# A first product by seven block products in the second half, groups of four feature tiles, and block sums kept in DRAM

## The chip, the cores and the metric

The program runs on one core of one Trainium2 chip. A core has a matrix engine (TensorE, "PE" in the profile; its weight loads are "PEld"), a vector engine (DVE), a scalar engine (ACT), GpSimd (POOL), the queue engine SyncE (SP) and 16 DMA engines. The metric is the device time of one execution in microseconds (us). A matmul is named by what streams through the array: "128x512" is a matmul of 512 columns, whose 128x128 stationary operand has been loaded by an LDWEIGHTS of its own.

## The reference, cut to what matters

```python
xn = layernorm(x)                                   # x = A_q, [2048, 576]
# conv branch
for t in range(4):                                  # short causal convolution of k, per channel
    k_shift += k_pad[:, t:t + S, :] * shift_k[:, 3 - t]
kv = k_shift * v
y = irfft(rfft(kv, 4096) * rfft(ssm_k, 4096))[:2048] + kv * ssm_D
branch_a = xn * y
# dense branch
h = relu(xn @ w1)                                   # w1 [576, 4608]
branch_b = h @ w2                                   # w2 [4608, 576]
return x + branch_a + branch_b
```

All of it is fp32. The kernel writes an operand of a matrix product as a sum of a high and a low part, and makes the product as three matmuls, high x high, high x low and low x high, that add up in one PSUM group.

## The kernel before, in words

**Dense branch.** The 2048 rows are four blocks of 512, two per half, and each half goes through all of W1 and W2. The 4608 features are 12 chunks of three feature tiles of 128 (`FT = 3`). For a chunk and a block, `mm1` (line 334) makes one feature tile of h, transposed, from 14 matmuls of 512 columns: 4 x 3 for the first 512 of the 576 input features, and 2 for the last 64, whose high and low part lie stacked on 128 partitions. ACT then writes the high part of relu(h) (`hh`, line 339), and DVE the low part (`ll`, line 340). `mm2` (line 358) takes 128 rows and 288 output columns: 9 matmuls (three feature tiles, three products) make one PSUM group, which DVE adds to the sum in SBUF (`acc`, line 362 for block 0, whose rows take 1/std on the way, line 366 for the others). That is 384 such adds. The weights come by DMA (`r`, lines 288 to 297); ACT makes their high parts (lines 306 and 315), POOL the low ones (line 277).

**The rows of the second half** are loaded, normalised and transposed by `make_xT` (line 269) in the last chunk of the first half, about 500 us into the program.

**Conv branch.** `conv` (line 408 on) is a generator that runs beside the dense branch: four stages of a long FFT, here called fk (the filter's first stage, lines 392 to 399), fx (the short convolution and the signal's first stage), fm (both second stages, the product and the way back, lines 553 to 617) and fo (the last stage and the gate, lines 656 to 703). In fx, each of 16 steps takes on DVE: one multiply by the first tap (line 483), three multiplies `e` (line 486), three adds (line 487), the gate by v (line 492), and two stacked splits `xs` (line 392), and for these the matmuls `psf<-xs` (line 398, 8 of 288 columns per step). ACT takes these out of PSUM (line 399).

**What sets the order.** There is one instruction stream for each engine. `tick(cost)` is called after each few matmuls of the dense branch. It counts their columns and, when the conv branch is behind its share, takes the generator's next step. A step yields its weight (`W_FK`, `W_FX`, `W_FM`, `W_FO`), or a negative number, which is a pause in columns of dense work. So these weights say how many dense matmuls stand between two conv matmuls. Each engine then takes its instructions strictly in this order and waits on semaphores. `here()` and `issue_after` set an instruction's place on ACT and DVE behind a named one.

**SP's queue.** It issues nearly all loads in program order. The filter comes in 16 loads `kt` (line 421) of 64 partitions x 36 x 32 elements with runs of 128 bytes, spaced by `KT_GAP` in columns of dense work. The weights of the next chunks lie among them.

Of the kernel before, what the change touches and what calls it, by code (L numbers as in the profile page):

```python
# [17 lines left out]
P = 128  # L18
# [8 lines left out]
FT = 3  # L27
FC = FT * P
NCHUNK = DFF // FC
# [15 lines left out]
W_MM1 = 14 * 512  # L45
W_MM2 = FT * 6 * NH
PAUSE = 16000
START = 4000
PAUSES = 16
SHARE = 0.985  # L50
# [3 lines left out]
W_FK, W_FX, W_FM, W_FO = 1.4, 4.1, 1.26, 2.4  # L54
KD = 36
KT_GAP = 6000
FFT_TOTAL = N_FK * W_FK + N_FX * W_FX + N_FM * W_FM + N_FO * W_FO

SPLITS = {(0, 1): ((1, 0),), (0, 2): ((1, 1),), (1, 0): ((1, 2), (2, 0)), (1, 1): ((2, 1),),
          (1, 2): ((2, 2),)}  # L60
SPLITS0 = {(1, 0): ((1, 0), (1, 1)), (1, 1): ((1, 2), (2, 0)), (1, 2): ((2, 1), (2, 2))}
FFN_TOTAL = NCHUNK * NB * (FT * W_MM1 + BT * W_MM2)

# [45 lines left out]
def h3_ffn_kernel(ctx: ExitStack, tc, x, k, v, shift_k, ssm_k, ssm_D, w1, w2, fwd, inv, mid, out):  # L109
# [8 lines left out]
    hp = ctx.enter_context(tc.tile_pool(name="hp", bufs=2 * FT))  # L118
    xp = ctx.enter_context(tc.tile_pool(name="xp", bufs=2))
    dram = ctx.enter_context(tc.tile_pool(name="dram", bufs=1, space=DRAM))  # L120
    ps_h = ctx.enter_context(tc.tile_pool(name="ps_h", bufs=2, space=PSUM))
# [11 lines left out]
    fin = dram.tile([HT // 2, P, 2, D], F32, name="fin")  # L133

# [21 lines left out]
    def load_x(t, tag, bufs, **queues):  # L156
        pair = xp.tile([P, 2, D], F32, tag=tag, name=f"{tag}{t}", bufs=bufs)
        move(pair, x, slice(t, t + 2), **queues)
        return pair

    def load_acc(t, **queues):
        pairs[t] = load_x(t, "acc", HT // 2, **queues)
        acc[t], acc[t + 1] = pairs[t][:, 0, :], pairs[t][:, 1, :]
# [27 lines left out]
    xT = {}  # L191
    done = {}

    def xT_tiles(b):
        hi = xp.tile([P, 4, 512], F32R, tag="xhi", name=f"xhi{b}")
        lo = xp.tile([P, 4, 512], F32R, tag="xlo", name=f"xlo{b}")
        hl = xp.tile([P, 512], F32R, tag="xhl", name=f"xhl{b}")
        xT[b] = (hi, lo, hl)

    def split_x(b, c, ps):  # L200
        hi, lo, hl = xT[b]
        if c < 4:
            last = nc.scalar.activation(hi[:, c, :], ps, AF.Copy)
            nc.vector.tensor_tensor(lo[:, c, :], ps, hi[:, c, :], OP.subtract)  # L204
            return last
        else:
            done["act"] = nc.scalar.activation(hl[:64, :], ps[:64, :], AF.Copy)
            done["dve"] = nc.vector.tensor_tensor(hl[64:, :], ps[:64, :], hl[:64, :],
                                                  OP.subtract)

    def first_xT(srcs):

        xT_tiles(0)
# [4 lines left out]
        behind = None  # L218
        for t in range(BT):
            if t % 2 == 0:  # L220
                pair = xp.tile([P, 2, D], F32, tag="xn", name=f"xn{t}", bufs=BT // 2)
            xn = pair[:, t % 2, :]
# [13 lines left out]
        for c in range(5):  # L236
            last = split_x(0, c, ps[c])
            if c == 1:
                with tc.issue_after(last.ins):
                    split_w1(0, 1)  # L240
# [5 lines left out]
    def make_xT(b, srcs, in_place=False):  # L246

        xT_tiles(b)
        t0 = b * BT
        for t in range(t0, t0 + BT):  # L250
            at = done["acc"] if in_place else lows[2 * (t - t0) // BT]
            with tc.issue_after(at.ins):
                stats(t, srcs[t])
        with tc.issue_after(at.ins):
            inv_std(t0, BT)
        xn = []
        for t in range(t0, t0 + BT):
            if in_place:
                xn.append(srcs[t])
            else:  # L260
                if t % 2 == 0:
                    pair = xp.tile([P, 2, D], F32, tag="xn", name=f"xn{t}", bufs=BT // 2)
                xn.append(pair[:, t % 2, :])
            normalized(xn[-1], srcs[t], t)
        for c in range(5):
            w = min(P, D - c * P)
            ps = fft_psum()
            for i in range(BT):
# [576 lines left out]
```

## Time and profile before

| | |
|---|---|
| time, median of 3 runs | 1087.06 us (1085.4 to 1087.46) |
| span of the profiled execution | 1084.4 us |
| TensorE matmuls | 1070.8 us busy, 6537 instructions |
| TensorE weight loads | 977.2 us busy |
| VectorE | 732.5 us busy, 1213 instructions |
| ScalarE | 585.0 us busy, 1184 instructions |
| GpSimd | 261.9 us busy, 218 instructions |
| granted TensorE clock | 0.997 |
| moved by DMA | 150.79 MB |

The profiled execution's span lies 2.7 us under the median of the runs. Matmuls overlap in the records (a record is longer than the distance from one start to the next), so a matmul's cost is read from start to start, and the busy share of PE says only that PE nearly always had a matmul under way. The page's parts by line and by wait name a helper's line where one records many operations; lines 392 and 398 each serve two stages, and the tile's name (ks or xs) tells them apart.

### The profile page before, as it was taken

What the parts mean: (1) busy time and instruction counts of PE and PEld (TensorE: products, weight loads), DVE (VectorE), ACT (ScalarE), POOL (GpSimd) and SP (SyncE); (2) the same over time, 40 slices, a digit from 0 to 9 for tenths busy, and PEclk for the clock granted to TensorE, in tenths of its full rate; (3) what the DMA queues carried; (4) which work ended last, traced back from release to release, by engine and by line L of the source; (5) the groups of instructions that cost most, each with busy time, mean ns of one, the idle gap of its engine ahead of it and who ended that gap; (6) DMA issues with size and microseconds to landing.
All of it is one profiled execution on the core that took longest, in us unless ns stands there. A gap on an engine that the chain in (4) does not pass through costs nothing.

```text
span 1084.4 us, 17301 instructions
## 1 busy us (share of the span) xinstructions
PE 1070.8 (99%) x6537; PEld 977.2 (90%) x6537; DVE 732.5 (68%) x1213; ACT 585.0 (54%) x1184; POOL 261.9 (24%) x218
## 2 busy tenths in 40 slices
PE   8999999999999999999999999999999999999998
PEld 5889899998999999999999999899999999999998
DVE  5423677949998777677666676666656666876774
ACT  4221587823443323333388787888788864543430
POOL 4131222412312322312213031211113032332410
PEclk9999999999999999999999999999999999999999
DMA  9950345664644525325564343434344227745524
GB/s 217 181 145 27 119 147 190 195 185 133 187 138 136 153 77 164 117 60 171 190 182 135 99 135 99 135 99 136 92 143 141 80 103 221 201 130 143 164 81 110
DMA packets 112255, 150.79 MB, mean 139 GB/s; under 512 B 45261, under 2 KB 62927, under 8 KB 112172
## 3 DMA queue, kind: packets, MB, share of 16 engines
q1 hardware_dynamic: 103884, 135.50, 42.0%
q0 software_dynamic: 7968, 13.44, 4.8%
q8 instruction: 52, 0.85, 0.3%
q10 hardware_dynamic: 320, 0.74, 0.3%
q14 instruction: 31, 0.25, 0.1%
HBM read 114.26 MB, written 35.39 MB: 138 GB/s over the span
## 4 chain that ended last, share of the span: by engine, by line
PE 90%; DMA 4%; SPq 2%; DVE 2%; ACT 1%; issue 1%; POOL 0%; ACTq 0%; DVEq 0%
PE pso L358 40%; PE psh L334 39%; PE psf L562 7%; PE psf L398 3%; DMA r<-in_w 3%; SPq L421 2%; PE psf L700 1%; PE psf L701 1%; DMA k-1_2414<-in_k 1%; DMA sk<-in_shift_k 0%; PE psf L269 0%; DVE lok L553 0%; POOL l L277 0%; DVE k L611 0%; DVE lox L553 0%
## 5 line engine op out<-in xcount | busy, mean ns | idle before, releaser
L277 POOL TENSOR_TENSOR l<-r,h 128x640 fp32r<-128x640 f32 (+1 forms) x144 | 224.4, 1563 | 621.8 <-ACT h L306 448.3
L358 PE MATMUL pso<-h,hh 128*128 128x288 f32 x1152 | 337.3, 295 | 3.7 <-ACT hh L339 2.7
L358 PE MATMUL pso<-l,hh 128*128 128x288 f32 x1152 | 338.5, 295 | 0.0
L358 PE MATMUL pso<-h,ll 128*128 128x288 f32 x1152 | 337.7, 295 | 0.0
L334 PE MATMUL psh<-xhi,h 128*128 128x512 f32 x576 | 226.5, 394 | 1.1 <-DVE ll L340 1.1
L334 PE MATMUL psh<-xlo,h 128*128 128x512 f32 x576 | 226.5, 393 | 0.0
L334 PE MATMUL psh<-xhi,l 128*128 128x512 f32 x576 | 225.8, 392 | 0.0
L358 PEld LDWEIGHTS pso<-h,hh 128*128 128x128 f32 x1152 | 215.8, 188 | 10.4 <-ACT hh L339 3.4
L358 PEld LDWEIGHTS pso<-l,hh 128*128 128x128 f32 x1152 | 216.3, 188 | 5.8
L358 PEld LDWEIGHTS pso<-h,ll 128*128 128x128 f32 x1152 | 216.0, 188 | 0.6
L366 DVE TENSOR_TENSOR acc<-pso,acc 128x288 f32<-128x288 f32 x288 | 128.6, 451 | 75.1 <-PE pso L358 72.1
L339 ACT ACTIVATE hh<-psh 128x512 fp32r<-128x512 f32 x144 | 85.6, 595 | 169.1 <-PE psh L334 168.2
L340 DVE SCALAR_TENSOR_TENSOR ll<-psh,hh 128x512 fp32r<-128x512 f32 x144 | 99.0, 687 | 109.8 <-ACT hh L339 109.5
L334 PEld LDWEIGHTS psh<-xhi,l 128*128 128x128 f32 x576 | 108.4, 188 | 20.3
L334 PEld LDWEIGHTS psh<-xhi,h 128*128 128x128 f32 x576 | 108.4, 188 | 17.1 <-DVE ll L340 1.4
L334 PEld LDWEIGHTS psh<-xlo,h 128*128 128x128 f32 x576 | 108.6, 188 | 15.5 <-DVE xlo L204 0.4
L315 ACT ACTIVATE h<-r 128x576 fp32r<-128x576 f32 x72 | 48.9, 682 | 73.4 <-DMA r<-in_w 46.9
L362 DVE SCALAR_TENSOR_TENSOR acc<-pso,rstd,acc 128x288 f32<-128x288 f32 x96 | 48.3, 512 | 27.5 <-PE pso L358 26.5
L392 DVE TENSOR_TENSOR ks<-kt,ks 64x288 fp32r<-64x288 f32 x64 | 57.6, 901 | 3.3 <-ACT ks L391 1.3
L399 ACT ACTIVATE zx<-psf 128x288 f32<-128x288 f32 x64 | 25.8, 407 | 59.3 <-PE psf L398 38.9
L334 PE MATMUL psh<-xhl,l 128*128 128x512 f32 x144 | 56.4, 392 | 0.0
L334 PE MATMUL psh<-xhl,h 128*128 128x512 f32 x144 | 56.2, 391 | 0.0
(109 smaller groups left out, 1451.2 us busy)
## 6 DMA issues: line engine op xcount, KB each, us to landing
r<-in_w SPq DMA_DIRECT2D x24, 864.0 KB, 5.3
r<-in_w SPq DMA_DIRECT2D x23, 768.0 KB, 6.1
zk<-zk SPq DMA_DIRECT2D x32, 288.0 KB, 2.5
zx<-zx SPq DMA_DIRECT2D x32, 288.0 KB, 2.6
ztk<-zk SPq DMA_DIRECT2D x32, 288.0 KB, 3.0
ztx<-zx SPq DMA_DIRECT2D x32, 288.0 KB, 2.8
zy<-vo SPq DMA_DIRECT2D x32, 288.0 KB, 2.1
zo<-zy SPq DMA_DIRECT2D x32, 288.0 KB, 3.0
```

The lines of the kernel that those rows point to most:

```text
L277: return nc.gpsimd.tensor_tensor(dst, src, hi, OP.subtract)
L315: nc.scalar.activation(h2, r2[:, j, :], AF.Copy)
L334: nc.tensor.matmul(ps, a, m, start=i == 0, stop=i == len(seq) - 1)
L339: done["act"] = nc.scalar.activation(hh, ps, AF.Relu)
L340: lows.append(nc.vector.scalar_tensor_tensor(ll, ps, 0.0, hh, op0=OP.max, op1=OP.subtract))
L358: nc.tensor.matmul(ps[:, :NH], a[:, cols], m[:, dc], start=n == 0, stop=n == 3 * FT - 1)
L362: done["acc"] = nc.vector.scalar_tensor_tensor(acc[t][:, dc], ps[:, :NH], rstd[:, t:t + 1], acc[t][:, dc], op0=OP.mult, op1=OP.add)
L366: done["acc"] = nc.vector.tensor_tensor(acc[t][:, dc], ps[:, :NH], acc[t][:, dc], OP.add)
L392: nc.vector.tensor_tensor(dst[other], src[own], dst[own], OP.subtract)
L398: nc.tensor.matmul(ps[:, :NH], w[:, u, n, :], stk, start=n == 0, stop=n == 1)
L399: nc.scalar.activation(z, ps[:, :NH], AF.Copy)
L562: nc.tensor.matmul(ps[:, :NH], a, m[:, cols], start=n == 0, stop=n == 2)
```

## The change

**Feature tiles and groups.** `FT` is 2, so the 4608 features are 18 pairs of tiles ("n" in the code counts both halves' pairs, 0 to 35). The first half makes its first product as before (line 512, 14 matmuls of 512 columns per tile). The second product (`unit`, line 575) now takes the tiles of two pairs at once: 12 matmuls make one PSUM group, and only the first and the last pair of a half go alone. That leaves 304 adds to `acc` (lines 579 and 583) where there were 384.

**Seven products.** In the second half `quad` makes both tiles of a pair for a block of 512 rows. The first 512 input features, the two tiles and the two halves of 256 rows are taken as a 2x2 block product in Winograd's form: seven block products of 6 matmuls of 256 columns (two input blocks of 128, three split products), and the last 64 input features as before, 4 matmuls of 512 columns. That is 46 matmuls where there were 28 of 512 columns. Between the block products ACT copies two of them from PSUM (`m5`, line 538, and line 539, PSUM to PSUM), and DVE adds twice (lines 543 and 546). One bank of PSUM per tile is used in place of two rotating ones.

**Sums of weights.** For the second half POOL makes the block sums of W1 (`sum_w`, four adds per pair), and `split_group` splits the originals and the sums: ACT and POOL then split 16 blocks of 128x128 per pair where a pair of the first half has 10, in five pieces.

**Sums of rows.** `later_xT` loads, normalises and transposes the rows of the second half during the first, from the third pair on, one small step at a time; DVE makes their block sums, ACT and DVE split them, and they are stored to DRAM (`kept`, 7.9 MB over both blocks: 2048 + 2048 + 3072 + 512 floats on 128 partitions, twice). `fetch` (line 376) reads them back. In SP's order of instructions the two loads of the sums `t` (1.57 MB each) and the last of the stores stand between the loads of k and v for the fx stage's third and fourth step; the rest (`b1`, `b2`, `xr`) is loaded at the change of halves.

**Conv branch.** Its instructions are the same. The weights in `tick` are now 1.5, 3.5, 2.1 and 2.9 where they were 1.4, 4.1, 1.26 and 2.4, the share .96 where it was .985, and `KT_GAP` 5000 where it was 6000. Several buffers are one fewer (`ks` 3 for 5, `xs` 3 for 4, `k` 5 for 6, `zo` 3 for 4), and the constants are loaded in single pieces.

The diff, cut to its core:

```diff
-FT = 3
+FT = 2
...
-SHARE = 0.985
+SHARE = 0.96
...
-W_FK, W_FX, W_FM, W_FO = 1.4, 4.1, 1.26, 2.4
+W_FK, W_FX, W_FM, W_FO = 1.5, 3.5, 2.1, 2.9
 KD = 36
-KT_GAP = 6000
+KT_GAP = 5000
...
+    def later_xT(b):
...
+        for kp in range(2):
+            ps = turned(2 * kp, xn)
+            with here():
+                nc.scalar.activation(e0, ps, AF.Copy)
...
+            nc.sync.dma_start(to["b2"][:, 0, :, kp], b2)
+            yield
+            with here():
+                split(b11, to["b1"][:, 0, :, kp, r12[0]])
+            yield
+            with here():
+                tt(v[:, r12[0]], b12, b11, OP.subtract)
+                split(v[:, r12[0]], to["b1"][:, 0, :, kp, r12[1]])
+            yield
...
+    def fetch(s, names):
+        for name in names:
+            t = operand(s, name)
...
+            nc.sync.dma_start(f32(t), kept[name][s])
...
+    def sum_w(n, k):
...
+        dst, a, b, op = ((s13[:, :, left], one[:, :, right], two[:, :, right], OP.add),
+                         (s24[:, :, left], s13[:, :, left], one[:, :, left], OP.subtract),
+                         (s13[:, :, right], one[:, :, left], one[:, :, right], OP.subtract),
+                         (s24[:, :, right], two[:, :, left], s24[:, :, left], OP.subtract))[k]
+        nc.gpsimd.tensor_tensor(dst, a, b, op)
...
+    def quad(n, s, m):
+
+        first, other = slice(0, HR), slice(HR, 512)
+        pb, pa = bank(m, f"psb{n}_{s}"), bank(1 - m, f"psa{n}_{s}")
+        run_seq(pb[:, other], product(n, s, "s1", "t1"), True)
+        run_seq(pb[:, first], product(n, s, "a11", "b11"))
+        m5 = xp.tile([P, HR], F32, tag="m5", name=f"m5_{n}_{s}", bufs=1)
+        nc.scalar.activation(m5, pb[:, other], AF.Copy)
+        done["act"] = nc.scalar.activation(pa[:, first], pb[:, first], AF.Copy)
+        yield
+        run_seq(pa[:, first], product(n, s, "a12", "b21"))
+        run_seq(pb[:, first], product(n, s, "s2", "t2"))
+        nc.vector.tensor_tensor(pa[:, other], pb[:, first], m5, OP.add)
+        yield
+        run_seq(pb[:, first], product(n, s, "s3", "t3"))
+        nc.vector.tensor_tensor(pb[:, other], pb[:, first], m5, OP.add)
+        run_seq(pa[:, other], product(n, s, "s4", "b22"))
+        run_seq(pa, rest(n, 0, s))
+        relu(n, s, 0, pa)
+        yield
+        run_seq(pb[:, first], product(n, s, "a22", "t4"))
+        run_seq(pb, rest(n, 1, s))
+        relu(n, s, 1, pb)
+        yield
...
+    def phase(ns, s, b, last):
+        order = [(i, h) for h in range(2) for i in range(BT)]
...
+        work.extend((len(ns), (ns, s, b, i, h, last)) for i, h in order)
+
+    def fill():
+        room = 2
+        while work and work[0][0] <= room:
+            size, args = work.pop(0)
+            unit(*args)
+            room -= size
...
+    for q, (n, s) in enumerate(visits):
+        half, m = divmod(n, NPAIR)
+        b = half * HB + s
+        second = q % 2
+        parts = quad(n, s, q % 2) if half else None
+        for st in range(4):
+            if half:
+                next(parts)
+            elif st % 2 == 0:
+                mm1(n, s, st // 2)
...
+            if half:
+                tick(W_STAGE[st])
+            if q > 3:
+                next(ahead, None)
+            fill()
+        if m == NPAIR - 1 and not half:
+            fetch(s, ("b1", "b2", "xr"))
+        if n == NPAIR - 2 and not half:
+            for _ in ahead:
+                pass
+            fetch(s, ("t",))
```

**Three places in the order of instructions.** TensorE in the second half (`psh` is the PSUM of the first product, `pso` that of the second). Before, in chunk 17 of 24:

```order
L334 MATMUL psh_2_0_8446<-xhi_5194,h_17_0_7998 128x512
L334 MATMUL psh_2_0_8446<-xlo_5195,h_17_0_7998 128x512
L334 MATMUL psh_2_0_8446<-xhi_5194,l_17_0_7999 128x512
L334 MATMUL psh_2_0_8446<-xhi_5194,h_17_0_7998 128x512
L334 MATMUL psh_2_0_8446<-xlo_5195,h_17_0_7998 128x512
L334 MATMUL psh_2_0_8446<-xhi_5194,l_17_0_7999 128x512
L334 MATMUL psh_2_0_8446<-xhi_5194,h_17_0_7998 128x512
L334 MATMUL psh_2_0_8446<-xlo_5195,h_17_0_7998 128x512
L334 MATMUL psh_2_0_8446<-xhi_5194,l_17_0_7999 128x512
L358 MATMUL pso_11_1_8416<-h_16_0_7609,hh_2_0_7868 128x288
L358 MATMUL pso_11_1_8416<-l_16_0_7610,hh_2_0_7868 128x288
```

And changed, in pair 22 of 36, around the fifth and sixth block product (`psb` and `psa` are the two tiles' banks, `t` the kept sums, `b` the rows, `xr` the last 64 features; "x6" is six such matmuls in a row):

```order
L575 MATMUL pso_12_1_8234<-w_22_1_8063,ll_1_1_7965 128x288
L575 MATMUL pso_13_1_8287<-w_21_1_7663,hh_1_0_7705 128x288 x2
L575 MATMUL pso_13_1_8287<-w_21_1_7663,ll_1_0_7706 128x288
L575 MATMUL pso_13_1_8287<-w_21_1_7663,hh_1_1_7754 128x288
L488 MATMUL psb_0_8005<-t_5556,g_2_7709 128x256 x6
L488 MATMUL psa_0_8006<-b_0_6127,g_2_7709 128x256 x6
L488 MATMUL psa_0_8006<-xr_6129,g_3_7758 128x512 x2
L575 MATMUL pso_13_1_8287<-w_21_1_7663,hh_1_1_7754 128x288
L575 MATMUL pso_13_1_8287<-w_21_1_7663,ll_1_1_7755 128x288
L575 MATMUL pso_13_1_8287<-w_22_1_8063,hh_1_0_7917 128x288 x2
L575 MATMUL pso_13_1_8287<-w_22_1_8063,ll_1_0_7918 128x288
```

The matmuls of 512 columns have become matmuls of 256, in runs of 6, with second products between the runs; what a run waits for (ACT's copies, DVE's adds) has the time of the matmuls ahead of it.

VectorE in the fx stage, one of 16 steps (`e`, `c`: taps and their sum, `xs`: the split for the matmuls, `acc` and `ll`: dense branch). Before:

```order
L340 SCALAR_TENSOR_TENSOR ll_0_2_2958<-psh_0_2_2931,hh_0_2_2957 128x512
L366 TENSOR_TENSOR acc_220<-pso_6_0_2961,acc_220 128x288
L366 TENSOR_TENSOR acc_220<-pso_6_1_2972,acc_220 128x288
L486 TENSOR_TENSOR e_2_2987<-k_2426,sk 128x576
L487 TENSOR_TENSOR c_2939<-c_2939,e_2_2987 128x576
L366 TENSOR_TENSOR acc_220<-pso_7_0_2990,acc_220 128x288
L486 TENSOR_TENSOR e_3_3001<-k_2418,sk 128x576
L487 TENSOR_TENSOR c_2939<-c_2939,e_3_3001 128x576
L366 TENSOR_TENSOR acc_220<-pso_7_1_3004,acc_220 128x288
L492 TENSOR_TENSOR c_2939<-c_2939,v_2880 128x576
L392 TENSOR_TENSOR xs_0_3042<-c_2939,xs_0_3042 64x576
L392 TENSOR_TENSOR xs_1_3056<-c_2939,xs_1_3056 64x576
```

And changed, for the same step:

```order
L711 TENSOR_TENSOR c_3018<-k_2969,sk 128x576
L715 TENSOR_TENSOR c_2905<-c_2905,e_2_2946 128x576
L495 SCALAR_TENSOR_TENSOR ll_1_1_3281<-psh_1_1_3252,hh_1_1_3280 128x512
L714 TENSOR_TENSOR e_3_2957<-k_2337,sk 128x576
L715 TENSOR_TENSOR c_2905<-c_2905,e_3_2957 128x576
L579 SCALAR_TENSOR_TENSOR acc_98<-pso_2_1_3284,rstd,acc_98 128x288
L720 TENSOR_TENSOR c_2905<-c_2905,v_2855 128x576
L714 TENSOR_TENSOR e_1_3034<-k_2852,sk 128x576
L579 SCALAR_TENSOR_TENSOR acc_98<-pso_3_1_3305,rstd,acc_98 128x288
L715 TENSOR_TENSOR c_3018<-c_3018,e_1_3034 128x576
L619 TENSOR_TENSOR xs_0_2990<-c_2905,xs_0_2990 64x576
L619 TENSOR_TENSOR xs_1_3004<-c_2905,xs_1_3004 64x576
```

The ten instructions of a step are the same; between two steps' `xs` there now stand fewer instructions of the dense branch, since there are fewer dense matmuls between two conv matmuls.

SyncE near the start, from the filter's first load on (`r`: weights, named by chunk or pair; `xn`, `rows`: rows of the second half). Before:

```order
L421 DMA kt<-in_ssm_k 64x36x32 x10
L288 DMA r_1_223<-in_w 128x4x384
L290 DMA r_1_223<-in_w 64x384 x2
L421 DMA kt<-in_ssm_k 64x36x32 x4
L297 DMA r_1_239<-in_w 128x3x576
L421 DMA kt<-in_ssm_k 64x36x32 x2
L152 DMA xn_4990<-in_x 64x1152 x2
L152 DMA xn_4993<-in_x 64x1152 x2
L288 DMA r_2_470<-in_w 128x4x384
```

And changed:

```order
L648 DMA kt<-in_ssm_k 64x36x32 x7
L394 DMA r_1_227<-in_w 128x4x256
L396 DMA r_1_227<-in_w 64x256 x2
L403 DMA r_1_0_234<-in_w 128x2x288
L648 DMA kt<-in_ssm_k 64x36x32
L403 DMA r_1_1_239<-in_w 128x2x288
L648 DMA kt<-in_ssm_k 64x36x32 x2
L154 DMA rows_651<-in_x 64x1152 x4
L648 DMA kt<-in_ssm_k 64x36x32 x6
L394 DMA r_2_451<-in_w 128x4x256
L396 DMA r_2_451<-in_w 64x256 x2
```

The weights of pair 1 now stand behind seven `kt` loads where those of chunk 1 stood behind ten, and those of pair 2 (`r_2`) behind all sixteen, as those of chunk 2 did.

557 lines of the change are left out of this document (357 added, 200 removed).

## The prediction

> **What bounds the kernel now.** I read the page's busy times and the chain of waits first.
>
> ```profile
> span 1084.4 us, 17301 instructions
> PE 1070.8 (99%) x6537; PEld 977.2 (90%) x6537; DVE 732.5 (68%) x1213; ACT 585.0 (54%) x1184; POOL 261.9 (24%) x218
> PE 90%; DMA 4%; SPq 2%; DVE 2%; ACT 1%; issue 1%; POOL 0%; ACTq 0%; DVEq 0%
> ```
>
> TensorE is busy throughout and is 90% of the chain that ended last, so the span is the sum of its matmuls plus a few stalls. DVE's 68% is an average; stage by stage (windows of fx, fx, fm, fm, fo) it is something else:
>
> ```profile
> core 0: us, PE busy (x) PEld busy (x) DVE busy (x) ACT busy (x) POOL busy (x), PEclk, DMA share, GB/s
> 245.00:330.00 85.00, 85.00 (x516) 77.72 (x517) 79.74 (x116) 33.56 (x62) 24.66 (x18) 1.00 0.49 147
> 330.00:516.00 186.00, 186.00 (x1132) 170.18 (x1131) 137.70 (x217) 63.66 (x118) 45.84 (x36) 1.00 0.43 128
> 529.00:700.00 171.00, 169.68 (x1061) 156.47 (x1060) 111.16 (x181) 132.27 (x290) 37.49 (x24) 1.00 0.44 140
> 700.00:877.00 177.00, 177.00 (x1119) 164.42 (x1118) 112.48 (x195) 145.52 (x322) 30.74 (x20) 1.00 0.36 109
> 886.00:1041.00 155.00, 155.00 (x950) 142.26 (x949) 111.15 (x195) 69.24 (x138) 45.23 (x46) 1.00 0.58 171
> ```
>
> At the start of fx DVE works 94% of the time (79.74 of 85), and TensorE never waits for it, by little; in fm ACT works 77 to 82%. Those are the two places with no room.
>
> Matmuls are priced from start to start, from the timeline of TensorE:
>
> ```profile
> 312.10 0.39 PE L334 MATMUL psh<-xhi,h 128*128 128x512 f32 x1
> ...
> 314.84 0.39 PE L334 MATMUL psh<-xhl,h 128*128 128x512 f32 x1
> 300.65 0.30 PE L358 MATMUL pso<-h,hh 128*128 128x288 f32 x1
> ...
> 302.90 0.29 PE L358 MATMUL pso<-h,ll 128*128 128x288 f32 x1
> 244.90 0.40 PE L358 MATMUL pso<-h,hh 128*128 128x288 f32 x1 [0.94 <-DVE acc L366]
> 244.90 0.19 PEld L358 LDWEIGHTS pso<-h,hh 128*128 128x128 f32 x1 [1.36 <-DVE acc L366]
> 245.00 0.19 PEld L358 LDWEIGHTS pso<-l,hh 128*128 128x128 f32 x1
> ```
>
> The first pair is 12 matmuls apart: 2.74 / 12 = 0.2283 us for 512 columns. The second is 17 apart: 2.25 / 17 = 0.1324 us for 288. Between them a column costs 0.0959 / 224 = 0.000428 us, and about 0.009 us is fixed. The last two rows show the first weight loads after a stall: they follow each other at 0.10 us, when nothing else holds them.
>
> **The seven products.** A pair of tiles and a block took 28 x 0.2283 = 6.39 us. Now it takes 42 matmuls of 256 columns and 4 of 512. No row has 256 columns; along the line of the two rows above it is 0.1324 - 32 x 0.000428 = 0.119 us, which I take, since 288 is near. So 42 x 0.119 + 4 x 0.2283 = 5.91 us, 0.48 less, and 36 times (18 pairs, two blocks) 17.3 us less. The bounds: without the fixed part it is 256 x 0.000428 = 0.110 us, and the saving 31 us; at the price of 288 columns it is 0.1324 us, and it would lose 3 us.
>
> The Trainium skill has two rules on this. "TensorE: Matmul & The Clock Gate", section "LDWEIGHTS (loading the stationary operand)", gives a load as its columns over 1.2, so 107 ns for 128, whatever the rows; the spacing of 0.10 us above agrees, and by it a 256-column matmul still hides its load, with 12 ns to spare. The same page, section "The mechanism" of its Part 3, says that a load overlaps a running matmul only in another row group; by that rule load and stream would add up, to some 220 ns for 256 columns by its figures, but the 0.1324 us of 288 columns already shows load and stream side by side, so I give it no weight.
>
> All other matmuls stay as many as they were, 4416 of 288 columns among them. The saved adds (80 of 384) and the regrouping free DVE, not TensorE.
>
> **The fx stage.** Here the change takes away cover. The conv weights are new, and the dense work is put differently: from the order of TensorE's instructions, seven steps of fx (first matmul on xs0 to first on xs7) held 380 matmuls of 288 columns and 189 of 512 before, 50.3 + 43.1 = 93.5 us, or 13.4 us a step. Twelve steps now hold 474 and 224, 62.8 + 51.1 = 113.9 us, or 9.5 us a step. DVE's part of a step is unchanged. Its groups in the window from 245 to 330 us:
>
> ```profile
> L487 DVE TENSOR_TENSOR c<-c,e 128x576 f32<-128x576 f32 x20 | 16.4, 821 | 0.4
> L486 DVE TENSOR_TENSOR e<-k,sk 128x576 f32<-128x576 f32 x16 | 15.4, 963 | 0.1
> L392 DVE TENSOR_TENSOR xs<-c,xs 64x576 fp32r<-64x576 f32 x14 | 11.1, 790 | 3.4 <-ACT xs L391 3.1
> L366 DVE TENSOR_TENSOR acc<-pso,acc 128x288 f32<-128x288 f32 x19 | 8.4, 450 | 1.1 <-PE pso L358 1.0
> L340 DVE SCALAR_TENSOR_TENSOR ll<-psh,hh 128x512 fp32r<-128x512 f32 x12 | 8.2, 684 | 0.1
> L362 DVE SCALAR_TENSOR_TENSOR acc<-pso,rstd,acc 128x288 f32<-128x288 f32 x16 | 8.0, 509 | 0.1
> L492 DVE TENSOR_TENSOR c<-c,v 128x576 f32<-128x576 f32 x7 | 7.9, 1130 | 0.1
> L483 DVE TENSOR_TENSOR c<-k,sk 128x576 f32<-128x576 f32 x7 | 6.2, 888 | 0.0
> L486 DVE TENSOR_TENSOR e<-k-3_2406,sk 128x576 f32<-128x576 f32 x1 | 1.6, 1621 | 0.0
> L486 DVE TENSOR_TENSOR e<-k-1_2414,sk 128x576 f32<-128x576 f32 x2 | 1.5, 750 | 0.0
> L486 DVE TENSOR_TENSOR e<-k-2_2410,sk 128x576 f32<-128x576 f32 x2 | 1.5, 749 | 0.0
> ```
>
> Three things come out. The rows add up to 86.2 us where the window has DVE busy for 79.74: records overlap, and a row's time counts 0.925 times. The mean e takes (15.4 + 1.6 + 1.5 + 1.5) / 21 = 0.952 us. And each xs waits 3.1 / 14 = 0.22 us for ACT's half.
>
> Between the xs of step 0 and step 12 DVE's order now has 36 e, 36 sums, 12 multiplies, 12 gates, 24 xs, 16 ll and 32 acc (16 with rstd). By the rows: 34.3 + 29.6 + 10.7 + 13.6 + 19.0 + 10.9 + 7.2 + 8.1 = 133.4 us, times 0.925 is 123.4, and 24 x 0.22 for ACT makes 128.7 us. TensorE offers 113.9 us of work in that time. So DVE falls behind by 14.8 us, and TensorE, which takes its matmuls in order, waits for xs. The same account of before (21 e, 21 sums, 7 multiplies, 7 gates, 14 xs, 13 ll, 36 acc: 85.1 us against TensorE's 93.5) has DVE ahead, as the trace does. Behind the waiting matmul stand the dense matmuls, so nothing covers it; from step 13 on dense work is 13 us a step and the wait ends.
>
> The lead at the first step goes too:
>
> ```profile
> 224.93 0.42 PE L398 MATMUL psf<-ks,wk 128*128 128x288 f32 x2
> 241.66 0.76 DVE L486 TENSOR_TENSOR e<-k-1_2414,sk 128x576 f32<-128x576 f32 x1 [5.36 <-DMA k-1_2414<-in_k]
> 252.45 1.54 DVE L392 TENSOR_TENSOR xs<-c,xs 64x576 fp32r<-64x576 f32 x2 [0.80 <-ACT xs L391]
> 260.94 0.43 PE L398 MATMUL psf<-xs,wx 128*128 128x288 f32 x2
> ```
>
> Before, the last ks matmul began about 225.2 us, the k rows came 16.5 us later, the first xs was done at 253.2, 28.0 us after ks, and TensorE wanted it at 260.9. Now 99 matmuls of 288, 56 of 512 and 12 short ones stand between, 27.2 us: the lead of 7.7 us is gone and the first wait is about 1 us; with the kept sums' stores and loads on SP's queue among those of k and v I take 2. Together 17 us. The bounds: a contended e took 1.62 us and a free one 0.75; if all ten instructions of a step took 0.75 (x 0.925), DVE would need 6.9 + 0.4 + 2.0 for the dense ones = 9.3 us a step, would keep up with 9.5, and 2 to 3 us of the start remain. With no overlap of records (133.4 + 5.3, against 113.9) it is 25 and 2, so 27.
>
> The Trainium skill ("SBUF — State Buffer", section "🔬 SBUF: two separate sides") says that a DVE instruction with two inputs in SBUF and a GpSimd instruction that reads SBUF lock each other out whole. The rows of 1.62 against 0.75 us fit that, and GpSimd's splits per feature are as many as before, so by it the slow share stays and DVE does not get faster.
>
> **The second half.** Each of the 36 products puts two copies on ACT and two adds on DVE between matmuls. The nearest ACT row is
>
> ```profile
> L399 ACT ACTIVATE zx<-psf 128x288 f32<-128x288 f32 x23 | 9.2, 406 | 14.1 <-PE psf L398 12.5 <-issue 1.5
> ```
>
> so two copies are some 0.8 us, and the adds 0.45 us each by the acc rows. In the order, the second product's matmuls between the runs give 1.6 us at the least and 2.8 us in the middle for the copies, and 3.2 us in the middle for the adds, 0.5 at the least. ACT is 77 to 82% busy in fm and often has a piece or two of 0.4 us ahead of the copies. I take 0.1 us for each of 36, so 4; bounds 0 and 9 (0.25 us each).
>
> **The start.** SP's queue paces the first 60 us:
>
> ```profile
> 12.66 23.96 SPq L421 DMA_DIRECT2D kt<-in_ssm_k  x10
> 48.47 1.37 SPq L297 DMA_DIRECT2D r<-in_w  x1
> 58.53 0.53 SPq L288 DMA_DIRECT2D r<-in_w  x1
> 56.69 0.61 PE L358 MATMUL pso<-h,hh 128*128 128x288 f32 x1 [2.51 <-ACT hh L339]
> ```
>
> A kt takes 2.4 us, and the second W2 load, issued at 48.47, left TensorE 2.51 us idle. Now pair 1's weights come after seven kt, but pair 2's behind all sixteen, about when they did before (58.5), and pair 2 is wanted at some 57 us of TensorE's time. The old stall goes, one of about the same size comes: +1, from -2 to +5. The kept sums' making costs TensorE nothing: its steps hang behind dense adds, and the freed 80 adds of 0.45 us outweigh them in DVE's total.
>
> **Sum.** 1084.4 - 17.3 + 17 + 4 + 1 = 1089.1 us, and with the 2.7 us that the median lies above the profiled span, 1092 us.
>
> **Rivals.** (A) DVE keeps up in fx: a step below 9.5 us, so the stall is 3 us and the second half's waits 3: 1084.4 - 17.3 + 3 + 3 + 1 + 2.7 = 1077. For it: 94% is not 100%, and the 0.75 us rows; against it: the account above, which fits before. It decides for faster as long as the fx stall stays under about 10 us. (B) In between, a stall of about 12 us: no change, 1087. (C) A 256-column matmul costs what one of 288 does: 1084.4 + 3 + 17 + 4 + 1 + 2.7 = 1112. For it is only that no row shows 256 columns; against it the straight line and the free load of 0.10 us. (D) ACT's copies wait behind fm's evictions by 0.4 us in each product, one piece: 36 x 0.4 = 14 us in place of 4, so 1102.
>
> **Chances.** The forecast 0.40, D 0.08 and C 0.06, all slower: 0.54. A 0.34, faster. B 0.12, no change (under 0.2%, some 2 us, a measurement of this kernel can't be told from none). The forecast's own range, a fx stall of 9 to 27 us, is 1084 to 1102. As A holds a third, the range reaches down to 1073 (A with the 256-column matmul at 0.117 us and no waits in the second half), and up to 1105, past D; C and the ends below A stay out.
>
> **What would show it.** In the changed profile: 256-column matmuls 0.119 us apart; idle time on TensorE before `psf<-xs` of 15 us or more in steps 1 to 13, released by DVE xs, with DVE above 95% busy there (right) or under 5 us (A); in fm and fo, idle time before the runs of 256 released by ACT's copies of 4 us in all, 14 for D. The prediction is wrong if fx runs at 9.5 us a step without waits, or if the runs of 256 do not come at 0.119 us.

## The result, and the profile after

The changed kernel takes 1094.49 us (median of 4 runs, 1092.36 to 1096.2), the kernel before in the same comparison 1086.37 us. The ratio is 1.0074, with a 95% interval of 1.0056 to 1.0093: slower by 0.7%. The prediction was 1092 us, slower, with a range of 1073 to 1105.

The page of the changed kernel: span, busy times, the chain of waits by engine and by line.

```profile
span 1094.4 us, 19562 instructions
PE 1064.2 (97%) x7185; PEld 997.5 (91%) x7185; DVE 751.4 (69%) x1245; ACT 629.8 (58%) x1349; POOL 390.3 (36%) x395
PE 77%; DVE 13%; DMA 5%; SPq 3%; issue 2%; ACT 0%; POOL 0%; DVEq 0%; ACTq 0%
PE pso L575 34%; PE psb L488 13%; PE psh L512 13%; PE psf L793 7%; PE psa L488 6%; DVE e L714 3%; SPq L648 3%; DVE c L715 2%; PE psf L625 2%; DMA r<-in_w 2%; DVE xs L619 2%; DVE c L711 1%; DVE c L720 1%; DMA sk<-in_shift_k 1%; DVE ll L495 1%
```

TensorE's part of the chain fell from 90% to 77%, and VectorE's rose from 2% to 13%, though VectorE's busy time hardly moved (68% to 69%). The lines of VectorE in the chain, 711 to 720 and 619, are the taps, the gate and the splits of fx. So the chain leaves TensorE mainly in one stage.

The seven products themselves, in the timeline of TensorE (start, time, group):

```profile
642.93 0.86 PE L488 MATMUL psb<-t,g 128*128 128x256 f32 x6
643.63 0.88 PE L488 MATMUL psa<-b,g 128*128 128x256 f32 x6
644.35 0.63 PE L488 MATMUL psa<-xr,g 128*128 128x512 f32 x2
```

Two runs of six matmuls take 0.70 and 0.72 us from start to start, 0.118 us a matmul (0.1178 is used from here on). A pair and a block then cost 42 x 0.1178 + 4 x 0.2283 = 5.86 us for the 6.39 before, and all 36 save 19.1 us.

**Where the time went.** The table gives TensorE's lag: the start of a matmul in the trace, less the sum of the start-to-start times of all matmuls ahead of it (0.2283, 0.1325, 0.1178 and 0.108 us for 512, 288, 256 and 128 columns). It counts idle time, the time lost to a slow clock, and the short waits that the busy records hide. Without lag the matmuls are 1059.7 us before and 1040.6 changed.

| lag in us at | first ks | last ks | first xs | start of fm | start of fo | last matmul |
|---|---|---|---|---|---|---|
| before | 14.5 | 15.1 | 16.3 | 17.0 | 20.1 | 20.5 |
| changed | 16.4 | 21.5 | 25.7 | 42.1 | 44.3 | 48.8 |

Stage by stage against before: the start 1.9 us more, the filter's stage fk 4.5 (5.1 for 0.6), fx with its beginning 18.7 (20.6 for 1.9), the second half from fm on 3.2 (6.7 for 3.5), the end after the last matmul 0.8. With the 19.1 saved: 1.9 + 4.5 + 18.7 + 3.2 + 0.8 - 19.1 = 10.0 us, the difference of the two profiled spans.

The rows of TensorE's waits, over the whole span, that bear on this (us, times, longest):

```profile
PE psf L625 <- DVE xs L619: 6.3, 7, 1.6
PE psf L625 <- ACT zx L626: 2.6, 4, 1.1
PE psf L625 <- DVE ks L619: 2.4, 1, 2.4
PE psf L625 <- issue: 1.9, 1, 1.9
PE psb L488 <- DVE psa L543: 1.2, 1, 1.2
```

The waits of fx lead. Those put down to the splits xs are a third of the 18.7 us; with the waits for ScalarE's `zx` and the one before the first xs matmul (the row "issue", where the view names no releaser) it is 10.8 us. A record of 288 columns lasts 0.296 us where the next could begin after 0.132, so this view hides some 0.16 us of every wait, and the slow clock it doesn't count. The lag has both. The stage itself, and its VectorE groups from 286 to 395 us:

```profile
core 0: us, PE busy (x) PEld busy (x) DVE busy (x) ACT busy (x) POOL busy (x), PEclk, DMA share, GB/s
264.00:268.00 4.00, 2.12 (x11) 1.92 (x10) 3.91 (x5) 3.52 (x7) 3.26 (x2) 0.67 1.02 366
268.00:272.00 4.00, 4.00 (x15) 3.54 (x14) 4.00 (x4) 0.66 (x2) 2.72 (x3) 0.50 0.96 322
272.00:276.00 4.00, 4.00 (x25) 3.60 (x24) 3.93 (x8) 0.86 (x2) 0.54 (x1) 0.98 0.83 227
286.50:395.00 108.50, 101.51 (x603) 90.57 (x602) 106.79 (x145) 48.15 (x96) 35.22 (x37) 1.00 0.60 178
```

```profile
L714 DVE TENSOR_TENSOR e<-k,sk 128x576 f32<-128x576 f32 x31 | 30.9, 995 | 0.3
L715 DVE TENSOR_TENSOR c<-c,e 128x576 f32<-128x576 f32 x31 | 25.1, 811 | 0.4
L619 DVE TENSOR_TENSOR xs<-c,xs 64x576 fp32r<-64x576 f32 x22 | 19.6, 892 | 0.7
L711 DVE TENSOR_TENSOR c<-k,sk 128x576 f32<-128x576 f32 x10 | 10.2, 1022 | 0.0
L720 DVE TENSOR_TENSOR c<-c,v 128x576 f32<-128x576 f32 x10 | 7.5, 753 | 0.2
```

VectorE works 106.79 of 108.5 us, 98%. There are 31 / 3 = 10.3 steps in that stretch, 10.5 us each, for which TensorE had 9.5 us of matmuls. At the first step TensorE stands, and the granted clock is 0.67 and 0.50 in two windows of 4 us there, back at 0.98 in the next.

Step by step the lag shows the two parts of the loss. It is 25.7 us at the first xs matmul, 28.4 at that of step 1, 34.7 at step 7, 41.7 at step 13 and 41.9 at step 15. So step 0, under the slow clock, loses 2.7 us, the steps from 1 to 13 lose 13.3, or 1.1 us each, and then the loss ends. Waits for one of the fewer buffers can't be what holds VectorE back here, as it stands idle for only 1.7 of the 108.5 us.

The start of fx has another limit. VectorE stands for the first rows of k:

```profile
252.55 0.76 DVE L714 TENSOR_TENSOR e<-k-1_2333,sk 128x576 f32<-128x576 f32 x1 [6.66 <-DMA k-1_2333<-in_k]
```

That is 17.3 us after the last ks matmul began at 235.3 us, where the prediction read 16.5 before, and the split that TensorE waits for began 12.2 us later, where it was 10.8.

The loss in fk, which the prediction did not have, is one place. VectorE's rows there, and TensorE's:

```profile
169.65 1.54 DVE L170 BATCH_NORM_STATS2 bn<-rows 128x6 f32<-128x288 f32 x4 [3.83 <-DMA rows<-in_x]
171.23 1.03 DVE L619 TENSOR_TENSOR ks<-kt,ks 64x288 fp32r<-64x288 f32 x1
172.31 0.53 PE L625 MATMUL psf<-ks,wk 128*128 128x288 f32 x2 [2.39 <-DVE ks L619]
```

VectorE waited 3.83 us for the fourth block's rows, with their statistics at the head of its queue. The filter's split ks stood behind them, and TensorE behind that. The wait is 2.39 us; the granted clock of 0.65 from 172 to 176 us and 0.92 from 176 to 180 adds 1.4 + 0.3 = 1.7 us.

### The profile page after: what moved, and what is told of

Same layout as the page of the kernel before. It is cut to its first block, busy times and chain, and to the rows that moved or that the text cites. A ratio compares the mean times of both kernels' runs of the same rounds, so it can differ in the third digit from the quotient of the medians.

```text
span 1094.4 us, 19562 instructions
## 1 busy us (share of the span) xinstructions
PE 1064.2 (97%) x7185; PEld 997.5 (91%) x7185; DVE 751.4 (69%) x1245; ACT 629.8 (58%) x1349; POOL 390.3 (36%) x395
## 4 chain that ended last, share of the span: by engine, by line
PE 77%; DVE 13%; DMA 5%; SPq 3%; issue 2%; ACT 0%; POOL 0%; DVEq 0%; ACTq 0%
PE pso L575 34%; PE psb L488 13%; PE psh L512 13%; PE psf L793 7%; PE psa L488 6%; DVE e L714 3%; SPq L648 3%; DVE c L715 2%; PE psf L625 2%; DMA r<-in_w 2%; DVE xs L619 2%; DVE c L711 1%; DVE c L720 1%; DMA sk<-in_shift_k 1%; DVE ll L495 1%
## 5 line engine op out<-in xcount | busy, mean ns | idle before, releaser
L575 PE MATMUL pso<-w,hh 128*128 128x288 f32 x2304 | 474.3, 296 | 3.2 <-DVE acc L583 1.4
L575 PEld LDWEIGHTS pso<-w,hh 128*128 128x128 f32 x2304 | 375.1, 188 | 12.3 <-DVE acc L583 1.8
L383 POOL TENSOR_TENSOR g<-r,g 128x256 fp32r<-128x256 f32 (+2 forms) x145 | 166.5, 1154 | 463.9 <-ACT g L412 385.7
L575 PE MATMUL pso<-w,ll 128*128 128x288 f32 x1152 | 330.3, 296 | 0.5 <-DVE ll L495 0.5
L512 PE MATMUL psh<-b,g 128*128 128x512 f32 x864 | 222.7, 399 | 2.9 <-DVE ll L495 1.6
L575 PEld LDWEIGHTS pso<-w,ll 128*128 128x128 f32 x1152 | 213.9, 189 | 1.8 <-DVE ll L495 0.8
L512 PEld LDWEIGHTS psh<-b,g 128*128 128x128 f32 x864 | 158.3, 191 | 32.9 <-ACT b L217 1.9
L383 POOL TENSOR_TENSOR w<-r,w 128x576 fp32r<-128x576 f32 x72 | 114.1, 1586 | 52.5 <-ACT w L474 52.3
L488 PE MATMUL psb<-t,g 128*128 128x256 f32 x648 | 94.6, 281 | 1.4 <-DVE psa L543 1.2
L488 PEld LDWEIGHTS psb<-t,g 128*128 128x128 f32 x648 | 85.1, 188 | 3.5 <-DVE psa L543 1.8
L619 DVE TENSOR_TENSOR ks<-kt,ks 64x288 fp32r<-64x288 f32 x64 | 50.4, 787 | 21.3 <-ACT ks L618 20.1
```

The costliest lines, as they stand in the source:

```text
L383: return nc.gpsimd.tensor_tensor(dst, src, hi, OP.subtract)
L488: nc.tensor.matmul(ps, a, m, start=start and i == 0, stop=i == len(seq) - 1, skip_group_check=not start)
L512: nc.tensor.matmul(ps, a, m, start=i == 0, stop=i == len(seq) - 1)
L575: nc.tensor.matmul(ps[:, :NH], a, m, start=c == 0, stop=c == len(seq) - 1)
L619: nc.vector.tensor_tensor(dst[other], src[own], dst[own], OP.subtract)
```

## The experiments

Theory 1: fx is bound by VectorE, since the new order gives TensorE less work per step than VectorE needs. Theory 2: fx is bound by the transfers on SP's queue, where the kept sums stand among k's and v's loads. Each kernel is given as a ratio to the kernel before, measured beside it on the same chip, where that took 1084.0 to 1084.8 us. All are edits of the changed kernel. Stage by stage readings come from one profiled execution of each kernel.

**two_taps**

```diff
             def tap(t, n):

-                if t >= T:
+                if t >= T or n >= 2:
                     return
```

> The changed kernel without the third and fourth tap of the short convolution (two of the three e and of the sums are left out in each fx step, so the result lacks these two taps). Nothing else is changed. Theory 1 (VectorE bounds fx): a step's VectorE work falls from 10.7 to 7.4 us by the account of the prediction, and TensorE's largest lag from 16.4 to 4.6 us, so about 12 us less: 1082 us, and idle time on TensorE before psf<-xs of 2 us or less. Theory 2 (the stall in fx comes from the transfers on SP's queue, the kept sums among those of k and v): these are as many as before, so 1094 us.

Measured: 1082.55 us, ratio 0.9983 (0.9969 to 0.9997). Fx, from the last ks to fm, lost 8.2 us of lag (19.4 to 27.6) for 20.6. VectorE's window:

```profile
265.00:425.00 160.00, 158.48 (x960) 144.34 (x960) 107.09 (x150) 68.02 (x140) 53.00 (x58) 1.00 0.64 194
```

VectorE is busy 67%, at about the same DMA share (0.64 for 0.60), and TensorE 158.48 of 160 us. The transfers were left as they were, so theory 2 falls as the cause of most of the loss. Of the 8.2 us that remain, 2.8 lie ahead of the first xs, where k's rows are waited for as in the changed kernel; the larger gaps of TensorE end at 257.8 us (2.2 us) and 290.7 us (1.0 us), in the first five steps. The order of TensorE's matmuls moved with this edit: the first four steps hold 5.5 to 6.6 us of matmuls each, less than VectorE's 7.4, and lose 2.9 us.

**paced**

```diff
-SHARE = 0.96
+SHARE = 0.9
-W_FK, W_FX, W_FM, W_FO = 1.5, 3.5, 2.1, 2.9
+W_FK, W_FX, W_FM, W_FO = 1.5, 3.1, 2.1, 2.9
...
+            yield -60000
+            clock["conv"] = min(clock["conv"], 0.0)
             for t in range(T):
```

> The changed kernel with its fx steps put further apart: one more pause ahead of the first step, the credit that the pauses left is dropped there, W_FX 3.1 and SHARE 0.90, so that a step has 11.1 us of TensorE's work for VectorE's 11.2. All instructions are the same, only their order differs. Theory 1 (VectorE bounds fx): the lag falls from 18 or 19 us to some 3, so 1094.5 - 15.5 = 1079 us, faster than the kernel before. Theory 2 (transfers): the loads still stand in the same order at the start of fx, where half of the lag or more stays: 1086 or more.

Measured: 1084.73 us, ratio 0.9998 (0.9985 to 1.0012). By the ratios this is 8 us less than the changed kernel, where 15.5 were expected, and it lies between what the two theories gave (1079, and 1086 or more). From the last ks to fm, 9.5 us are still lost (19.1 to 28.6) for 20.6. One place shows in VectorE's timeline:

```profile
277.09 1.01 DVE L714 TENSOR_TENSOR e<-k,sk 128x576 f32<-128x576 f32 x1
284.83 0.95 DVE L619 TENSOR_TENSOR xs<-c,xs 64x576 fp32r<-64x576 f32 x1 [6.73 <-ACT xs L618]
```

VectorE, in order, stands 6.73 us behind the split's other half on ScalarE, with the dense adds and the next taps queued there. What held up ScalarE is a transfer:

```profile
275.30 0.68 ACT L474 ACTIVATE w<-r 128x576 fp32r<-128x576 f32 x1
283.17 0.63 ACT L412 ACTIVATE g<-r 128x512 fp32r<-128x512 f32 x1 [7.19 <-DMA r<-in_w]
284.12 0.68 ACT L618 ACTIVATE xs<-c 64x576 fp32r<-64x576 f32 x1
```

ScalarE stood 7.19 us for weights. They were issued from 272.5 us on, next after a load of the kept sums (`t`, 1.57 MB, at 271.83), and landed 10 us later, where the medians of this kernel's weight loads are 3.3 and 5.4 us. So transfers have a part in what fx still loses here, 1.7 us of lag from step 0 to step 1; that the kept sums' load delayed the weights is not shown by a run of its own.

**plain_second**

```diff
-        if n + 1 < NPAIR:
+        if n + 1 < HALVES * NPAIR:
...
-                split(v[:, r12[0]], to["b1"][:, 0, :, kp, r12[1]])
+                split(b12, to["b1"][:, 0, :, kp, r12[1]])
...
-            if half:
-                next(parts)
-            elif st % 2 == 0:
+            if st % 2 == 0:
                 mm1(n, s, st // 2)
```

> The changed kernel with the first product plain in both halves (28 matmuls of 512 columns per pair and block in place of 42 of 256 and 4 of 512; the block sums of the rows are still made and stored, those of W1 are not). Theory: the seven products save 36 x (28 x 0.228 - 42 x 0.118 - 4 x 0.228) = 19 us of matmuls and cost some 3.5 us of waits in the second half; the account of fx gives 3.6 us less lag in this order. So 1094.5 + 19 - 3.5 - 3.6 = 1106 us. Rival: the waits of the seven products eat half of their saving, and this kernel comes out at 1098 or less.

Measured: 1108.79 us, ratio 1.0229 (1.0206 to 1.0252). Against the changed kernel's 1.0074 the seven products are worth 0.0155 x 1085 = 17 us. The rival falls. The lag from fm to the last matmul is 4.4 us (40.6 to 45.0) for the 6.7 of the changed kernel, and for 6.0 to 6.3 in the other kernels here that have the same second half (two_taps, late_rows, early_rows, no_gpsimd_in_fx). So the waits that the seven products bring are some 2 us of their 19.1.

**late_rows**

```diff
-        yield
-        yield
+        for _ in range(2 if b == HB else 4):
+            yield
```

> The changed kernel with two more steps between the load of the fourth block's rows and their statistics on VectorE, nothing else. Theory: the 2.39 us wait at 172 us, where the statistics stand at the head of VectorE's queue for a load that has not landed and the filter's split waits behind them, goes, and the slower clock after it: 3 to 4 us less, 1091 us. Rival: fx, which VectorE bounds, takes the time back, as the filter's stage only ends earlier: 1094 us.

Measured: 1093.67 us, ratio 1.0088 (1.0073 to 1.0103), as the changed kernel. The profile shows the same wait (2.40 us before the ks matmul at 172.75 us). VectorE's order had not moved: the statistics still stood behind the 31st split. The run says nothing on the theory.

**early_rows**

```diff
-        xr = hold[:, 4 * D:4 * D + 512].bitcast(F32R)
+        xr = e0.bitcast(F32R)
...
-        yield
-        yield
+        for _ in range(2 if b == HB else 7):
+            yield
...
-        nc.sync.dma_start(kept["xr"][s], hold[:, 4 * D:4 * D + 512])
+        nc.sync.dma_start(kept["xr"][s], e0)
...
-            if q > 3:
+            if q > 2:
                 next(ahead, None)
```

> The changed kernel with the fourth block's rows loaded well ahead of their statistics: the last features' sums are kept in the other scratch tile, so that the rows' tile comes free earlier, the making of the sums starts one visit earlier, and five more steps stand between the fourth block's load and its statistics. In the kernel late_rows the statistics had kept their place in VectorE's order, so it tested nothing. Theory: the 2.4 us wait of TensorE at 172 us and the slower clock behind it go, the filter's stage ends 4 us earlier, and with it all that follows in fx: 1094 - 4 = 1090 us. Rival: fx takes it back, since VectorE's and the loads' work there is as much: 1094 us.

Measured: 1089.56 us, ratio 1.0049 (1.0033 to 1.0065). The statistics find their rows (no idle time before them):

```profile
154.35 1.53 DVE L170 BATCH_NORM_STATS2 bn<-rows 128x6 f32<-128x288 f32 x4
155.91 0.90 DVE L619 TENSOR_TENSOR ks<-kt,ks 64x288 fp32r<-64x288 f32 x1
```

The filter's stage loses 1.1 us (15.5 to 16.6) for 5.1. Fx doesn't take it back: it loses 18.4 for 20.6. The gain is 0.0025 in the ratio against the changed kernel's own comparison and 0.0039 against late_rows', 3 to 4 us. The intervals keep this kernel apart from late_rows, but not from the changed kernel.

**paced_early** joins paced, with `yield -50000`, and early_rows; no other line differs.

> Both edits together: fx steps paced as in the kernel paced, with a pause of 50000 in place of 60000 columns (there the first splits were ready 6.7 us before TensorE took the ones ahead of them, and VectorE's adds stood behind the wait for a free buffer), and the rows' load ahead of their statistics. By the account of fx VectorE's step takes 11.1 us and TensorE's 11.2, the largest lag is 1 us. Theory (the two losses are separate): 1084.7 - 4 for the rows - 2 for the first step = 1079 us, faster than the kernel before. Rival (what is taken away at one place comes back at the next): 1084 us.

Measured: 1079.72 us, ratio 0.9953 (0.9939 to 0.9967), faster than the kernel before. The time is what the theory had, and the rival falls. The lag is 15.1, 16.2, 18.0, 24.3, 26.0 and 32.5 us at the table's six places. Fx loses 8.1 us, the second half 8.2, so the account's largest lag of 1 us in fx was too low. The 6.7 us that the expectation puts down to a free buffer were the wait of ScalarE for weights. That wait is there again (7.71 us, to 279.94), but VectorE's longest wait for a split's other half near it is now 2.24 us, and TensorE's wait 0.45 us.

**paced_tight** is paced_early with `yield -45000` and `W_FX` 3.2.

> As paced_early, with a pause of 45000 columns and W_FX 3.2, so TensorE reaches the first fx matmul some 4 us earlier, before its split is ready, and then has 11.4 us a step for VectorE's 11.1. Theory: the start of fx costs 3 to 4 us more than in paced_early and the later steps nothing, so 1081 us. Rival: the start waits for k's load in either case, and it is the same as paced_early within 1 us.

Measured: 1084.03 us, ratio 0.9992 (0.9981 to 1.0002): 4.3 us more than paced_early for the 2 expected. TensorE's first xs matmul came at 259.3 us for 262.9. The wait did not come there, as the theory had it (2.6 us of lag from the last ks for 1.8), but in the steps after it: from the first xs to fm 9.6 us were lost for 6.3, though the steps were set 0.2 us further apart. The rival, which had both starts alike, falls too. One of the later waits, 1.62 us before the xs matmul at 313.23, stands behind a wait of ScalarE for weights (5.32 us, to 311.67); for the rest the cause stays open.

**no_groups**

```diff
-        if second == 0:
-            phase([n] if m == 0 else [n - 1, n], s, b, last)
-        elif last:
-            phase([n], s, b, True)
+        phase([n], s, b, last)
```

> The changed kernel with every pair's second product alone, 6 matmuls to a PSUM group in place of 12, so that VectorE has 608 adds to acc where it had 304; nothing else. Theory (VectorE bounds fx): a step's VectorE work goes from 10.7 to 12.1 us, TensorE's part of a step in this order to 10.5, the largest lag from 16.4 to 21.3 us, and in the second half the adds stand among those of the seven products: 1094.5 + 5 + up to 5 = 1100 to 1105 us. Rival (VectorE has room outside fx and fx is bound by loads): 1095 us.

Measured: 1093.31 us, ratio 1.0084 (1.0054 to 1.0113): no slower than the changed kernel, with twice the adds. The theory's number fails here. In fx VectorE is busier still:

```profile
260.00:440.00 180.00, 171.36 (x974) 148.33 (x975) 177.83 (x268) 71.20 (x143) 56.61 (x58) 1.00 0.63 187
L714 DVE TENSOR_TENSOR e<-k,sk 128x576 f32<-128x576 f32 x29 | 24.1, 832 | 0.2
```

VectorE is busy for 177.83 of 180 us. From 285 to 400 us a step took 11.5 us of VectorE for TensorE's 10.5, so it fell behind by 1.0 us a step, as in the changed kernel (10.5 for 9.5), where the account had 1.6. The e were faster, 0.832 us for 0.995; why, no run shows. In the second half TensorE lost less, 4.0 us for 6.7. The account, a difference of two large sums with a price for each instruction, is right on which engine is behind and wrong on how far: it had a largest lag of 21.3 us, and from the first xs to fm 15.1 were lost (24.1 to 39.2).

**no_gpsimd_in_fx**

```diff
     def split_lo(dst, src, hi):
+        if stage["fx"]:
+            return nc.scalar.activation(dst, src, AF.Copy)
         return nc.gpsimd.tensor_tensor(dst, src, hi, OP.subtract)
```

> The changed kernel in which, during fx alone, the low parts of the weights are written by ScalarE as a copy in place of GpSimd's subtraction (so these low parts are wrong numbers; the instructions on the other engines and TensorE's order of matmuls stay). Theory (VectorE's instructions with two inputs in SBUF are held up by GpSimd's splits): e falls from a mean of 0.995 us to the 0.75 us of its free rows, the other taps and the gate likewise, a step's VectorE work from 10.6 us to some 9.4, below TensorE's 9.5, and of the 16 to 19 us lost in fx only the start's 3 to 4 stay: 1081 us. Rival (VectorE's slow rows have another cause, the transfers or SBUF itself): e stays near 1 us and the time at 1094 us, or above it for ScalarE's added work.

Measured: 1079.06 us, ratio 0.9951 (0.9933 to 0.9968). VectorE's groups from 286 to 395 us, beside those of the changed kernel above:

```profile
L718 DVE TENSOR_TENSOR e<-k,sk 128x576 f32<-128x576 f32 x35 | 26.3, 753 | 0.4
L719 DVE TENSOR_TENSOR c<-c,e 128x576 f32<-128x576 f32 x35 | 26.3, 752 | 0.4
L623 DVE TENSOR_TENSOR xs<-c,xs 64x576 fp32r<-64x576 f32 x24 | 18.1, 754 | 0.8
L724 DVE TENSOR_TENSOR c<-c,v 128x576 f32<-128x576 f32 x12 | 9.0, 754 | 0.2
L715 DVE TENSOR_TENSOR c<-k,sk 128x576 f32<-128x576 f32 x11 | 8.3, 750 | 0.0
```

Each of them has its free time of 0.75 us, with 35 / 3 = 11.7 steps in the stretch for 10.3. The ten instructions of a step took (26.3 + 26.3 + 18.1 + 9.0 + 8.3) / 11.7 = 7.5 us, in the changed kernel (30.9 + 25.1 + 19.6 + 10.2 + 7.5) / 10.3 = 9.1. Fx loses 3.1 us (21.3 to 24.4) for 20.6. In this kernel TensorE has the same matmuls in fx in the same order as in the changed kernel, step for step, and from step 1 to step 13 its lag grows by 0.9 us (23.1 to 24.0) for 13.3. The transfers are no fewer: the DMA share from 286 to 395 us is 0.66 for 0.60. So the rival falls. In the changed kernel GpSimd's splits in that stretch were

```profile
L383 POOL TENSOR_TENSOR g<-r,g 128x512 fp32r<-128x512 f32 (+1 forms) x11 | 13.9, 1266 | 38.0 <-ACT g L412 28.1 <-PE psf L625 9.9
L383 POOL TENSOR_TENSOR w<-r,w 128x576 fp32r<-128x576 f32 x6 | 11.1, 1856 | 1.1 <-ACT w L474 1.1
```

So 25 us of GpSimd on the weights' low parts in that stretch made VectorE's steps 1.6 us longer, and all but 3 us of TensorE's loss in fx hung on that. GpSimd's other work in the stretch, issuing the loads `wx`, is in both kernels (11.0 us, and 11.7 without the splits).

**paced_single**

```diff
+        if half:
+            phase([n], s, b, last)
-        if second == 0:
+        elif second == 0:
             phase([n] if m == 0 else [n - 1, n], s, b, last)
```

This edit comes on top of paced_early.

> paced_early with the second product of the second half alone per pair (6 matmuls to a group), groups of four tiles in the first half only. In no_groups TensorE lost 4.0 us in the second half where the changed kernel lost 6.7, and paced_early 8.2, although VectorE had twice the adds. Theory: the longer groups hold a bank of PSUM longer, and TensorE waits for the adds that free it; with short groups some 3 to 4 us less: 1076 us. Rival: the adds that come back fill VectorE in the last stage, where it is busy 80% of the time: 1080 us or more.

Measured: 1076.23 us, ratio 0.9930 (0.9909 to 0.9951). The lag from fm to the last matmul is 6.7 us (24.1 to 30.8) for 8.2: 1.5 us less, half of what was expected. The two ratios differ by 0.0023, 2.5 us, which their intervals don't keep apart for certain. It is the fastest kernel here that computes all, some 8 us under the kernel before.

## Why the prediction was right, point by point

**The seven products: right.** The line through 512 and 288 columns gave 0.119 us for 256, and 0.118 was measured; the saving is 19.1 us for 17.3. Rival C falls. On the Trainium skill ("TensorE: Matmul & The Clock Gate"): its 107 ns for a load of 128 columns (section "LDWEIGHTS (loading the stationary operand)") fits, as 0.118 us leaves it room. The sentence in its section "The mechanism" that a load overlaps a matmul only in another row group, taken by itself, does not hold for this kernel, where load and 256 columns together took 0.118 us.

**Fx: right in place and size.** 17 us were predicted (14.8 for VectorE's steps, 2 for the start), 18.7 measured against before. VectorE's step was put at 10.7 us and took 10.5; the steps from 1 to 13 lost 13.3 us, and the wait ended at step 13, as predicted. What the sum had mis-sized is the start: 4.2 us from the last ks to the first xs, where 1.2 were lost before, and then 2.7 us in step 0 under the slow clock, which no term stood for. Two taps fewer and no splits on GpSimd took most of the loss away, other pacing half of it, and the transfers were left as they were. So it is shown that VectorE set this stage's pace. Rivals A and B did not happen. One sign that the prediction named did not come as stated: 15 us or more of idle time released by xs would have shown it right, under 5 us rival A, and the view has 6.3 us. The lag decides it, which also has what the records hide.

**What VectorE's slow share is.** The prediction took it as given, from the row of 1.62 us beside 0.75, and cited the Trainium skill ("SBUF — State Buffer", section "🔬 SBUF: two separate sides") beside it. The run without GpSimd's splits agrees with it: with these gone from the stage, every tap takes 0.75 us in the mean, for 0.81 to 1.02 with them.

**The second half: right in size, wrong in cause.** 4 us were predicted for waits on ACT's copies and VectorE's adds; 3.2 us were measured. But the products' waits are some 2 us, and the longer groups of the second product probably had their share: without them the second half of one profile lost 2.7 us less. Rival D falls: no wait of TensorE on ScalarE's copies is long enough to appear.

**The start: right.** +1 was predicted, 1.9 measured. The old stall of 2.51 us went, and one of 1.56 us came at 62.58 us, behind a wait of ScalarE for weights of 8.21 us (to 60.69).

**The step that failed** is "the kept sums' making costs TensorE nothing: its steps hang behind dense adds, and the freed 80 adds of 0.45 us outweigh them in DVE's total". A total says nothing of one place in an in-order queue: the statistics of the fourth block stood at its head for a load that had not landed, TensorE waited 2.39 us behind them and had a slow clock after it, and fk lost 4.5 us more than before. With the load earlier fk lost 1.1 us in place of 5.1.

**The groups of four** were priced at nothing for TensorE. That they bring no time that can be measured is shown by no_groups (1.0084 for 1.0074, within both intervals); that they cost in the second half is indicated by that run's and paced_single's lag, and not shown.

In the span the sum came out 5.3 us low (1089.1 for 1094.4): the failed step 4.5, fx 1.7, the start 0.9 and the end 0.8 too low, the products 1.8 and the second half 0.8 too high. That the forecast of 1092 us was only 2.5 us low is in part luck: the profiled run was the slowest of the four (1096.2 us), so the median of the runs lies at the profiled span and not 2.7 us above it. The lower end of the range is also mis-added: rival A with 0.117 us and no waits in the second half comes to 1071 us by the prediction's own terms, not 1073. The measured time is far from it.

## What to carry to other kernels

When a change shortens one engine's work, look up who works beside it in each stage: an engine that is 94% busy there is the next bound, whatever its share of the whole span. Price such an engine's instructions from rows of that stage and not from their free time, and look for what slows them: here a third engine's light work, 25 us in 109, decided whether the change lost or gained (a ratio of 1.0074 with it, 0.9951 without). In an in-order queue, a wait for a load costs what stands behind it, so a load that is moved is placed by when it lands.

## What the runs showed of the hardware

- The taps on VectorE (128x576, two inputs in SBUF) took 0.75 us without GpSimd's splits in the stage, and 0.81 to 1.02 us in the mean with 25 us of these splits in 109 us. The gate, of the same shape, took 0.753 us in the mean even so.
- After TensorE had stood for 1.9 us at the start of fx, and again after the wait of 2.39 us in fk, the granted clock fell: to 0.67 and 0.50 in two stretches of 4 us there, and to 0.65 from 172 to 176 us. In the later stalls of fx, 1.6 us at the most, it was 1.00. The length of a stall alone does not decide it: in early_rows TensorE stood 2.45 us before 397.80 us and the clock was 1.00 from 394 to 406 us, and in late_rows it stood 0.95 and 0.56 us before 321.88 and 323.50 and the clock was 0.58 from 324 to 328 us.
- A run of matmuls of 256 columns goes at 0.118 us each, with a weight load for each.
